# Second MLP's weight words through ScalarE's leaky step, and a shorter reach for the written-out order

## The chip, the cores and the metric

The kernel runs on one core of one Trainium2 chip. The metric is the time of the whole program on the device, in microseconds (us), from the first instruction to the last write. Five engines work beside each other, each through its own queue in order: PE (TensorE, with its weight loads shown as PEld), DVE (VectorE), ACT (ScalarE), POOL (GpSimd) and SP (SyncE, which issues nearly all DMAs here).

## What is computed

Causal attention with a decay bias (4 batches, 8 heads, 576 positions, 64 per head), then two MLPs over its 2304 tokens, each 512 wide with 2048 in the middle. The first has a softplus in the middle, the second a quotient of two polynomials.

```python
x = attention(q, k, v, s)                    # 2304 x 512, fp32
h = x @ moe_w_in;  g = softplus(h);  x = g @ moe_w_out
h = x @ moe2_w_in
P = a0 + a1*h + a2*h*h + a3*h*h*h
Q = 1 + |b0|*|h| + |b1|*h*h
out = (P / (Q + 1e-6)) @ moe2_w_out
```

The four weight matrices come as 64-bit floats, so the kernel reads pairs of 32-bit words and builds fp32 values from them on the chip. All matrix products are made in three passes of a shorter format: a value is split into a high part (a rounded copy) and a low part (the value less its high part), and high by high, high by low and low by high are summed in PSUM.

## The kernel before

**Stages.** From 0 to about 200 us attention for the first tokens and the building of the first MLP's weights share the engines. Then the first MLP runs (token tiles T1 of 256 and 448 columns, 16 units of 128 middle rows each) with the rest of attention woven in, to about 625 us. The second MLP follows: its first tile (384 tokens) plainly, three tiles of 512 with a scheme that saves one product in eight, and the last tile (TAIL, 384 tokens) plainly again, from about 962 us to the end.

**A unit** of an MLP is `stage_a` (12 matmuls, x by the in-weights, L1095 to L1097), `stage1` to `stage3` (the function on ACT, DVE and POOL, ending with the high part `gh` on ACT and the low part `gl` on POOL, both seen as L1391 and L1393) and `stage_b` (the out-weights into `acc`, L1131 to L1133 in the first MLP, L1138 to L1140 in the second). In the first MLP L1197 is the DVE step that frees the PSUM bank of `h` in the tiles meant here; in the second it is L1209.

**Building weights.** `load_w` fetches 128 x 512 pairs of words. `conv_t(m, ff, half)` turns them into fp32 in a tile `tc` (three buffers), m is 0 for the first MLP's weights and 1 for the second's. `conv_hl` then takes the high part on ACT (L921) and the low part on POOL (L922). There are 32 such conversions for each MLP. Those of the second MLP are issued by `conv2_a` and `conv2_b` during units 65 to 96, which is the last two tiles of the first MLP and the start of the second; for each pair of converted in-weights `sum_make` (L986 to L989, four DVE steps) and `sum_split` (L997 on ACT, L998 on POOL) make and store sums that the saving scheme needs. Twelve of the 32 (the in-weights' half of units 0 to 11) go into buffers of the tag W, which the first MLP's last tile frees unit by unit.

For m = 0 the conversion is a DVE shift of the low word (L910), one ACT step (Prelu, which scales by one factor above zero and by another below, L911) on the high word in place, and one DVE step that shifts and joins (L912). For m = 1 it is a scaling on POOL in place (L914) and three DVE steps (L915, L916, L917). For either, the first step on the loaded words waits for the load.

**Order.** The program is traced in a hand-made sequence with priorities. Before the framework schedules it, a planner in the kernel (`Step`, `Planner`, `plan`) lays all instructions out over the engines with its own table of durations, six rounds by turns of start and due times, takes the round that ends soonest, and ties each engine's instructions into that order. `plan` leaves out of the ties every instruction whose planned start is at or after `UNTIL`, on the planner's own clock, which the trace doesn't show. With 2000.0 nothing is left out. What is left out keeps its data waits and its priority, and the framework places it.

Of the kernel before, what the change touches and what calls it, by code (L numbers as in the profile page):

```python
# [11 lines left out]
AF = mybir.ActivationFunctionType  # L12
ALU = mybir.AluOpType
# [52 lines left out]
SHARED = {("two", "wide"): 0.7, ("two", "thin"): 0.25, ("one", "wide"): 0.7, ("one", "thin"): 0.3,  # L66
          ("wide", "two"): 0.2, ("wide", "one"): 0.05, ("thin", "two"): 0.6, ("thin", "one"): 0.3}
HOLD, ROUNDS = 0.0, 6
UNTIL = 2000.0
DMA_RATE, DMA_LATENCY, LANES = 320e3, 1.9, 8  # L70


# [252 lines left out]
def plan(instructions, tied, until):  # L325
    p = Planner(instructions, tied)
    rank = [s.i.bass_priority for s in p.steps]
    best = None
    for _ in range(ROUNDS):
        total = p.forward(rank)  # L330
        if best is None or total < best[0]:
            best = total, p.lines, p.start
        rank = p.latest()
    _, lines, start = best
    return [[p.steps[k].i for k in line if start[k] < until] for line in lines.values()]
# [3 lines left out]
def moe_chain_kernel(ctx, tc, qk0, v0, qk, vv, s0, s, w1, w2, ab, out):  # L339
    nc = tc.nc  # L340
# [558 lines left out]
    def conv(m, ff, half, hi, lo):  # L899
        conv_hl(conv_t(m, ff, half), hi, lo)  # L900

    def conv_t(m, ff, half):
        r = raw64.pop((m, ff, half))
        lw = r[:, :, 0]
        hf = r.bitcast(F32)[:, :, 1]
        hw = r[:, :, 1]
        t = sb.tile([128, 512], F32, tag="tc", bufs=3, name="tc")
        ti = t.bitcast(I32)
        if m == 0:
            nc.vector.tensor_scalar(ti, lw, 29, None, op0=ALU.logical_shift_right)  # L910
            nc.scalar.activation(hf, hf, AF.Prelu, scale=2.0 ** -112, alpha=-(2.0 ** 32))  # L911
            nc.vector.scalar_tensor_tensor(ti, hw, 3, ti, op0=ALU.logical_shift_left, op1=ALU.bitwise_or)  # L912
        else:
            nc.gpsimd.tensor_scalar(hf, hf, 2.0 ** -112, 1.0, op0=ALU.mult, op1=ALU.mult)  # L914
            nc.vector.tensor_scalar(ti, hw, 3, None, op0=ALU.logical_shift_left)  # L915
            nc.vector.scalar_tensor_tensor(ti, hw, -2147483648, ti, op0=ALU.bitwise_and, op1=ALU.bitwise_or)  # L916
            nc.vector.scalar_tensor_tensor(ti, lw, 29, ti, op0=ALU.logical_shift_right, op1=ALU.bitwise_or)  # L917
        return t

    def conv_hl(t, hi, lo):  # L920
# [27 lines left out]
    def conv2_a(ff, half):  # L948
        t = conv_t(1, ff, half)
        c2_open.append((conv2_hl, (ff, half, t)))  # L950
        if half == 0:
            q, p = ff // 4, ff // 2 % 2
            pairs.setdefault((q, p), []).append(t)
            if ff % 2:
                pairs[q, p].append(sb.tile([128, 512], F32, tag="tc", bufs=3, name="tc"))
                c2_open.append((sum_make, (q, p)))
                c2_next.extend((sum_split, (q, p, n)) for n in range(2))
# [659 lines left out]

    for line in plan(nc.cur_bb.bb.instructions, tied, UNTIL):
        for prev, i in zip(line, line[1:]):
# [59 lines left out]
```

## Time and profile before

| | us |
|---|---|
| three runs | 1047.83, 1048.87, 1049.39 (median 1048.87) |
| the profiled execution, its own time | 1048.41 |
| its span in the trace | 1046.6 |
| PE busy in the span | 1005.5 |
| DVE busy | 846.5 |
| ACT busy | 785.6 |
| POOL busy | 506.7 |

The profiled execution lies 0.46 us below the median of the three, and its time is 1.8 us longer than its span. Busy times are those of the engine itself; waiting isn't in them. PE's busy time counts a matmul as busy also while it runs at the lower of its two clock levels, which the granted clock shows (1.00 is full speed, 0.50 the lower level).

### The profile page before, as it was taken

The numbers are of one execution on the slowest core, as the hardware profiler recorded it, in microseconds if no ns is written. First come the engines' busy times: TensorE is split into PE (matmuls) and PEld (weight loads), VectorE is DVE, ScalarE is ACT, GpSimd is POOL, SyncE is SP. The second block draws the span as 40 slices with busy tenths as digits, with TensorE's granted clock in tenths as the row PEclk, the third lists the DMA queues.
The fourth block names the chain that finished last, engine by engine and source line by source line (L and its number), as shares of the span: only waits on it lengthen the run. The fifth ranks groups of instructions, "written<-read, shape, count | busy, mean of one in ns | idle before, by whom it ended". The sixth has DMA issues, their size and how long they took to land. (4 is left out here: it accounts for less than half of the span.)

```text
span 1046.6 us, 18293 instructions
## 1 busy us (share of the span) xinstructions
PE 1005.5 (96%) x5924; PEld 902.2 (86%) x5924; DVE 846.5 (81%) x1815; ACT 785.6 (75%) x1620; POOL 506.7 (48%) x496
## 2 busy tenths in 40 slices
PE   6999999999999999999999978899999999999997
PEld 5889999989998888889999968688888898899895
DVE  5788987888987888886667899898889878878866
ACT  5998888887987777766566555778778888788765
POOL 2757654311211122234437876676567457455542
PEclk9999999999999999999999999999999999999999
DMA  8868565665555644337689987967645655654300
GB/s 242 299 237 274 180 223 178 201 196 153 169 179 153 203 138 152 97 136 235 215 261 332 330 276 255 357 215 271 195 162 186 215 181 175 201 175 147 121 1 31
DMA packets 103503, 207.93 MB, mean 199 GB/s; under 512 B 11632, under 2 KB 28848, under 8 KB 103408
## 3 DMA queue, kind: packets, MB, share of 16 engines
q1 hardware_dynamic: 100864, 202.60, 58.6%
q10 hardware_dynamic: 2544, 4.16, 1.6%
q8 instruction: 47, 0.77, 0.3%
q14 instruction: 48, 0.39, 0.1%
HBM read 163.25 MB, written 39.39 MB: 194 GB/s over the span
## 5 line engine op out<-in xcount | busy, mean ns | idle before, releaser
L616 POOL TENSOR_SCALAR PA<-PA,stat 128x384 f32<-128x384 f32 (+3 forms) x112 | 73.1, 659 | 164.0 <-DVE stat L615 64.8
L1095 PE MATMUL h<-xs,w1h 128*128 128x448 f32 (+1 forms) x360 | 123.1, 343 | 3.8 <-DVE e L1197 3.7
L1096 PE MATMUL h<-xs,w1h 128*128 128x448 f32 (+1 forms) x360 | 122.7, 341 | 0.0
L1097 PE MATMUL h<-xs,w1l 128*128 128x448 f32 (+1 forms) x360 | 122.3, 340 | 0.0
L1132 PE MATMUL acc<-gl,w1h 128*128 128x448 f32 (+1 forms) x352 | 119.1, 340 | 1.2 <-POOL gl L1393 1.2
L1133 PE MATMUL acc<-gh,w1l 128*128 128x448 f32 (+1 forms) x352 | 118.8, 340 | 0.1
L1131 PE MATMUL acc<-gh,w1h 128*128 128x448 f32 (+1 forms) x352 | 118.9, 341 | 0.0
L1260 POOL TENSOR_TENSOR gl<-PA,gh 128x512 fp32r<-128x512 f32 x48 | 63.7, 1328 | 70.1 <-issue 57.3
L613 ACT ACTIVATE PA<-PA,stat 128x384 f32<-128x384 f32 (+3 forms) x112 | 64.0, 572 | 16.2 <-DVE stat L596 14.1
L1095 PEld LDWEIGHTS h<-xs,w1h 128*128 128x128 f32 x360 | 67.9, 189 | 9.0 <-DVE e L1197 5.7
L1096 PEld LDWEIGHTS h<-xs,w1h 128*128 128x128 f32 x360 | 67.8, 188 | 3.7 <-DVE xs L1060 0.4
L1097 PEld LDWEIGHTS h<-xs,w1l 128*128 128x128 f32 x360 | 67.8, 189 | 3.2
L1132 PEld LDWEIGHTS acc<-gl,w1h 128*128 128x128 f32 x352 | 66.4, 189 | 4.6 <-POOL gl L1393 1.4
L1133 PEld LDWEIGHTS acc<-gh,w1l 128*128 128x128 f32 x352 | 66.2, 189 | 3.4 <-POOL w1l L922 0.3
L1131 PEld LDWEIGHTS acc<-gh,w1h 128*128 128x128 f32 x352 | 66.3, 189 | 3.1 <-ACT gh L1391 0.2
L1193 ACT ACTIVATE e<-h 128x448 f32<-128x448 f32 (+1 forms) x90 | 43.4, 482 | 32.2 <-PE h L1097 29.2
L1393 POOL TENSOR_TENSOR gl<-e,gh 128x256 fp32r<-128x256 f32 (+1 forms) x48 | 47.6, 992 | 29.9 <-ACT gh L1391 24.7
L1276 PE MATMUL acc<-w2b,gl 128*128 128x512 f32 x144 | 55.5, 397 | 2.0 <-POOL gl L1260 2.0
L1274 PE MATMUL acc<-w2b,gh 128*128 128x512 f32 x144 | 56.8, 394 | 0.0
L1275 PE MATMUL acc<-w2b,gh 128*128 128x512 f32 x144 | 56.7, 394 | 0.0
L596 DVE CUSTOM_DVE_ANT_0 PA<-at,mask 128x384 f32<-128x384 f32 (+3 forms) x100 | 50.4, 518 | 5.9 <-PE at L624 3.9
L623 PE MATMUL at<-ht 128*128 128x512 f32 (+3 forms) x156 | 53.5, 348 | 1.1 <-DVE stat L604 0.8
(362 smaller groups left out, 3325.8 us busy)
## 6 DMA issues: line engine op xcount, KB each, us to landing
wa<-wa_d SPq DMA_DIRECT2D x100, 512.0 KB
w1l<-l_d SPq DMA_DIRECT2D x138, 256.0 KB
raw<-in_w_dram SPq DMA_DIRECT2D x48, 512.0 KB
raw<-in_qk_dram SPq DMA_DIRECT2D x24, 384.0 KB
l_d<-w1l SPq DMA_DIRECT2D x32, 256.0 KB
raw64x<-in_w_dram SPq DMA_DIRECT2D x16, 512.0 KB
wa_d<-pt SPq DMA_DIRECT2D x16, 512.0 KB
wa_d<-w2a SPq DMA_DIRECT2D x24, 256.0 KB
```

Of the source, the lines that this page charges most:

```text
L613: nc.scalar.activation(pt[:, 0:n], pt[:, 0:n], AF.Exp, bias=mn, scale=-1.0, accum_out=stat[:, i, 1:2])
L616: nc.gpsimd.tensor_scalar(pt[:, 0:n], pt[:, 0:n], stat[:, i, 2:3], 1.0, op0=ALU.mult, op1=ALU.mult)
L1095: nc.tensor.matmul(h, wh[:, cs], xh, start=(k == 0), stop=False)
L1096: nc.tensor.matmul(h, wh[:, cs], xl, start=False, stop=False)
L1097: nc.tensor.matmul(h, wl[:, cs], xh, start=False, stop=(k == KD - 1))
L1131: nc.tensor.matmul(o, wh[:, cs], gh, start=first and not both, stop=False)
L1132: nc.tensor.matmul(o, wh[:, cs], gl, start=False, stop=False)
L1133: nc.tensor.matmul(o, wl[:, cs], gh, start=False, stop=last and (not both or m % 2 == 1))
L1260: nc.gpsimd.tensor_tensor(gl, bl.g, f(gh), op=ALU.subtract)
L1274: nc.tensor.matmul(acc[m], gh[:, cs], wh, start=first, stop=False)
L1275: nc.tensor.matmul(acc[m], gh[:, cs], wl, start=False, stop=False)
L1276: nc.tensor.matmul(acc[m], gl[:, cs], wh, start=False, stop=last)
```

## The change

`conv_t` loses its second branch: the weights of both MLPs are now converted as the first MLP's were. For each of the 32 conversions of the second MLP one POOL step and three DVE steps go, and two DVE steps and one ACT step come. `UNTIL` becomes 936.0, so that instructions which the planner starts at 936 us of its clock or later (nearly all of the last tile) are no longer tied in its order. The planner runs again over the changed list of instructions, so the order of the rest may change as well.

```diff
-UNTIL = 2000.0
+UNTIL = 936.0
...
-        if m == 0:
-            nc.vector.tensor_scalar(ti, lw, 29, None, op0=ALU.logical_shift_right)
-            nc.scalar.activation(hf, hf, AF.Prelu, scale=2.0 ** -112, alpha=-(2.0 ** 32))
-            nc.vector.scalar_tensor_tensor(ti, hw, 3, ti, op0=ALU.logical_shift_left, op1=ALU.bitwise_or)
-        else:
-            nc.gpsimd.tensor_scalar(hf, hf, 2.0 ** -112, 1.0, op0=ALU.mult, op1=ALU.mult)
-            nc.vector.tensor_scalar(ti, hw, 3, None, op0=ALU.logical_shift_left)
-            nc.vector.scalar_tensor_tensor(ti, hw, -2147483648, ti, op0=ALU.bitwise_and, op1=ALU.bitwise_or)
-            nc.vector.scalar_tensor_tensor(ti, lw, 29, ti, op0=ALU.logical_shift_right, op1=ALU.bitwise_or)
+        nc.vector.tensor_scalar(ti, lw, 29, None, op0=ALU.logical_shift_right)
+        nc.scalar.activation(hf, hf, AF.Prelu, scale=2.0 ** -112, alpha=-(2.0 ** 32))
+        nc.vector.scalar_tensor_tensor(ti, hw, 3, ti, op0=ALU.logical_shift_left, op1=ALU.bitwise_or)
         return t
```

## Rows read from the trace of the kernel before

**Rows 1.** The page's first part: busy us, share of the span, instructions.

```profile
PE 1005.5 (96%) x5924; PEld 902.2 (86%) x5924; DVE 846.5 (81%) x1815; ACT 785.6 (75%) x1620; POOL 506.7 (48%) x496
```

**Rows 2.** Busy us by stretch: length, PE, PEld, DVE, ACT, POOL, granted clock, DMA.

```profile
590.00:660.00 70.00, 59.95 (x288) 53.24 (x287) 65.54 (x79) 38.44 (x74) 50.00 (x41) 0.98 0.81 274
660.00:720.00 60.00, 56.27 (x290) 47.47 (x289) 52.57 (x75) 46.88 (x90) 43.53 (x35) 1.00 0.75 266
0.00:200.00 200.00, 183.52 (x1309) 170.40 (x1310) 162.68 (x494) 162.50 (x406) 113.75 (x138) 1.00 0.70 227
200.00:560.00 360.00, 359.39 (x2043) 324.20 (x2042) 282.16 (x768) 266.53 (x581) 97.68 (x125) 1.00 0.58 183
...
963.00:1032.00 69.00, 69.00 (x345) 61.90 (x343) 54.45 (x82) 49.90 (x96) 34.88 (x32) 1.00 0.15 49
```

**Rows 3.** PE's waits, 560 to 660: for whom, us, times, longest.

```profile
PE h L1095 <- DVE e L1197: 5.3, 4, 3.1
PE h L1095 <- DVE PA L1209: 2.7, 3, 1.7
PE acc L1138 <- ACT gh L1391: 1.9, 1, 1.9
```

**Rows 4.** PE's longest gap of these (timeline), and two stretches after it.

```profile
621.91 0.45 PE L1095 MATMUL h<-yt,w2a 128*128 128x384 f32 x1 [3.09 <-DVE e L1197]
...
622.00:624.00 2.00, 2.00 (x8) 1.90 (x9) 2.00 (x2) 1.94 (x5) 1.86 (x3) 0.68 1.01 376
624.00:626.00 2.00, 2.00 (x8) 1.87 (x7) 2.00 (x4) 1.05 (x2) 2.00 (x3) 0.50 0.95 337
```

**Rows 5.** DVE's groups by line, 590 to 660: count, busy us, mean ns.

```profile
L916 DVE SCALAR_TENSOR_TENSOR tc<-raw,tc 128x512 int32<-128x512 int32 x5 | 6.3, 1255 | 0.1
L917 DVE SCALAR_TENSOR_TENSOR tc<-raw64x,tc 128x512 int32<-128x512 int32 x5 | 5.4, 1080 | 0.1
L915 DVE TENSOR_SCALAR tc<-raw64x 128x512 int32<-128x512 int32 x5 | 5.1, 1021 | 0.0
...
L916 DVE SCALAR_TENSOR_TENSOR tc<-raw64x,tc 128x512 int32<-128x512 int32 x5 | 4.4, 885 | 0.1
...
L917 DVE SCALAR_TENSOR_TENSOR tc<-raw,tc 128x512 int32<-128x512 int32 x5 | 3.7, 741 | 0.1
...
L915 DVE TENSOR_SCALAR tc<-raw 128x512 int32<-128x512 int32 x5 | 3.6, 723 | 0.7 <-POOL raw L914 0.7
```

**Rows 6.** Single lines: groups 0 to 200, then whole span as min/median/max ns.

```profile
L912 DVE SCALAR_TENSOR_TENSOR tc<-raw,tc 128x512 int32<-128x512 int32 x32 | 27.5, 860 | 2.0 <-ACT raw L911 1.8
L910 DVE TENSOR_SCALAR tc<-raw 128x512 int32<-128x512 int32 x32 | 20.8, 656 | 2.8 <-POOL w1l L922 2.1 <-DMA raw<-in_w_dram 0.6
...
L911 ACT ACTIVATE raw<-raw x32: 646/667/694, 20.9 to 190.7; 128x512 f32<-128x512 f32 x32
...
L916 DVE SCALAR_TENSOR_TENSOR tc<-raw,tc x16: 674/833/1776, 410.8 to 641.1; 128x512 int32<-128x512 int32 x16
```

**Rows 7.** POOL: L914 by stretch (us, count), and its waits 390 to 660.

```profile
590.00:660.00 70.00, 6.64 (x8) 0.98 0.81 274
...
POOL raw L914 <- DMA raw<-in_w_dram: 20.3, 7, 8.2
POOL raw64x L914 <- DMA raw64x<-in_w_dram: 7.9, 6, 2.3
```

**Rows 8.** The end: PE's waits from 1000, then PE's and ACT's timeline.

```profile
PE acc L1138 <- ACT gh L1391: 2.4, 3, 1.0
PE acc L1140 <- POOL gl L1393: 0.8, 2, 0.4
...
1029.84 0.34 PE L1097 MATMUL at<-xl,wa 128*128 128x384 f32 x1
...
1030.22 0.71 ACT L1205 ACTIVATE tmp<-e,prm 128x384 f32<-128x384 f32 x1
1032.48 0.52 ACT L1391 ACTIVATE gh<-PA 128x384 fp32r<-128x384 f32 x1 [1.54 <-DVE PA L1222]
...
1033.97 0.47 ACT L1204 ACTIVATE e<-at 128x384 f32<-128x384 f32 x1
```

## Prediction, written before the changed kernel was run

> **What bounds the kernel now.** I read the busy times of the whole span first, then the same by stretch, then PE's waits in the stretches where PE is not full, then the engine that it waits for there. PE is busy 96% of the span, DVE 81%, ACT 75%, POOL 48% [rows 1], so the program as a whole is PE's, and a change that takes no matmul away can give back only PE's idle time and its time at the lower clock. By stretch [rows 2] PE is full from 200 to 560 (359.39 of 360 us) and from 963 to 1032 (69.00 of 69). It is idle at the start (16.5 us of the first 200), from 590 to 660 (70 less 59.95, 10.05 us), from 660 to 720 (3.73 us) and at the very end. In 590 to 660 another engine is the full one: DVE is busy 65.54 of 70 us, while ACT has 31.6 us free and POOL 20. PE's waits there name DVE: 5.3 us for L1197 and 2.7 us for L1209, the DVE steps that free the PSUM bank of h, and 1.9 us for a gh that itself stands behind DVE's L1222 [rows 3]. That makes 9.9 of the 10.05 us. After the longest gap, 3.09 us, the granted clock falls: 0.68 in the next 2 us and 0.50 in the 2 us after them [rows 4], which is the lower level of 1.2 GHz in place of 2.4. Together (2 x 0.32 + 2 x 0.50) this is 1.64 us of lost work beside the idle time. So what DVE's lateness costs from 590 to 660 is about 11.7 us, and this is the stretch in which ten of the 32 conversions run.
>
> **The conversion, DVE's part.** In this stretch ten conversions cost DVE 6.3 + 5.4 + 5.1 + 4.4 + 3.7 + 3.6 = 28.5 us [rows 5], 2.85 us each. The new form is in the trace already, for the first MLP: L912 27.5 and L910 20.8 us over 32 [rows 6], 48.3 / 32 = 1.51 us each, in a stretch in which POOL is busy 57% [rows 2]. In 590 to 660 POOL is busy 71%, and 62% once its 6.64 us for L914 are gone [rows 7], so 1.51 us fits. The upper bound of the relief is then 10 x (2.85 - 1.51) = 13.4 us. The lower bound is one undisturbed two-input step for each conversion, 0.674 us, the least of L916 [rows 6]: 6.7 us. Between them lies how much of DVE's lengthening (L916 takes 0.674 us at the least and 1.776 at the most for one shape) goes away with L914. I take a relief of 10 us, nearer to the first MLP's rows since they are the same two instructions beside the same POOL work.
>
> The Trainium skill (SBUF — State Buffer, section Who interferes with whom) says that DVE steps with two SBUF inputs and GpSimd steps lock each other out for a whole instruction. The lengths of L916 agree. By this rule L914's 6.64 us come off DVE's waiting at the most; with the 6.7 us of the removed step that would be 13.3 us, an estimate that meets the upper bound above.
>
> **What of that reaches PE.** DVE with 55 us of work in 70 would no longer be full, and PE's work there takes 59.95 us, some 58.3 at full clock. Not all idle goes: the steps still come in bursts (the four steps of the sums beside two conversions, then L1197), and the banks of h give PE little slack. I take 70% of the 10.05 us, 7.0 us. The lower clock came behind the longest gap; if that gap shrinks as the others do, most of the 1.64 us comes back, and I take 1.5. What comes late next is DVE still, at a lower load, then POOL's low parts and sums (43 us in 70). From 660 to 720 no conversion is left, but a smaller backlog enters it; of its 3.73 us I take none, and 1 us as a bound.
>
> **ACT's part.** 32 Prelu steps of 0.667 us [rows 6], 21.3 us. L911 varies from 646 to 694 ns although it stands between the attention's and the softplus' functions, so no table is switched for it. Ten fall into 590 to 660, 6.7 us against 31.6 us free; the others fall into a stretch where ACT is busy 266.53 of 360 us [rows 2]. I cost them at nothing as work: ACT's free time hides them, and if that cover were gone each 0.667 us would stand before an Abs, Exp or Ln of a unit. What they can cost is a wait. The first step on a loaded word pair waits for the load: POOL waited 20.3 us in 7 times and 7.9 us in 6 for it, once 8.2 us [rows 7]. This wait now stands in ACT's queue (and DVE's, whose first step reads the same load), with gh and the function steps of the first MLP behind it, for which PE waits. Bounds: 0 (the planner puts the step where the load has landed) and 8.2 us (the longest wait passed on whole). PE is full where these loads are made and units lie three deep between `stage_a` and `stage_b`, so a wait of a microsecond or two is covered; I take 1 us.
>
> The Trainium skill (ScalarE: Activation LUTs, rules for kernel authors) says to do relu and multiplications on VectorE and not on ScalarE. The rows show next to no difference for one step of this size: 0.667 us for L911, 0.656 us in the mean for the one-input L910 on DVE beside POOL's work [rows 6]. By the rule the scaling would go to DVE, ten such steps in the stretch where DVE is full; the relief would shrink by 6.6 us, and at 70% of it the time would be 1041 + 4.6 = 1045.6 us.
>
> **POOL's part.** 32 steps leave POOL. POOL is not full anywhere PE waits, so by itself this is worth nothing; its effect on DVE is counted above. One POOL wait moves: its low parts no longer queue behind L914.
>
> **The last tile.** From 963 to 1032 PE is full in the planner's order. Then it waits 2.4 us for gh and 0.8 us for gl [rows 8], 3.2 us. One cause is visible: the last unit's matmuls are issued by 1029.84 + 0.34, ACT ends its queue's work at about 1030.9, then waits for the gh of an earlier unit until 1032.48, and takes the last unit's Abs (L1204) only at 1033.97. Another order could take that Abs some 3 us earlier. So the bound on the good side is 3.2 us, and on the bad side there is none in the trace, since every instruction of it was tied; I bound it by letting each of the 16 units wait as the first late one does at the end (1.0 us, the longest for gh, and 0.4 for gl, half of the two waits): 16 x 1.4 = 22 us. DVE (54.45 of 69), ACT (49.90) and POOL (34.88) have time there, so any order that keeps three units in flight leaves PE full, and I take 0.
>
> **Sum.** Against the profiled execution: 1048.41 - 7.0 - 1.5 + 1.0 + 0 = 1040.9 us. The median lies 0.46 us above this execution: 1041.4, and I say 1041.
>
> **Rivals.** (a) The relief is there but little of it reaches PE: low parts, the sums on POOL, or the buffers of the tag W (freed unit by unit by the first MLP's last tile) hold the conversions, and PE's waits keep their size under other names. For it: POOL waits for ACT there as ACT does for DVE, a chain in which one link is shortened. Against it: 9.9 of 10.05 us of PE's waits name DVE directly or one step away. It would give a third of the 8.5 us: 1048.9 - 2.8 = 1046. (b) Nothing to measure: the planner lays the whole program out anew from a changed list, and what is gained from 590 to 660 is lost in the first 200 us, which hold 16.5 us of idle time in an order that would change, or in the last tile: 1047 to 1051. (c) Slower, by the last tile: the framework places a unit's `stage_b` on PE before its gl is there, and the next `stage_a` stands behind it in PE's queue. Its place is 963 to 1043, its price up to 1.4 us a unit, and from 8.5 / 1.4 = 6 late units on it eats the gain; with all 16 late the time is 1041 + 22 = 1063. Against it: DVE, ACT and POOL have a fifth to a half of their time free there. (d) Slower, by ACT's queue: three or more Prelu steps wait for loads as long as POOL's 8.2 us once did, with PE's gh behind them. Beyond a cover of some 5 us each (a guess: PE lost 0.61 us in all from 200 to 560 although POOL had that wait there) this is 3 x 3.2 = 10 us: 1051. (e) More than forecast: all 11.7 us, 1 us from 660 to 720 and 3.2 at the end: 1033. (f) That the change doesn't do what it says, with the leaky step slower than its rows or the planner keeping POOL's order, I leave out: the same function on the same shape runs 32 times in this trace.
>
> **How the numbers follow.** A measurement of this kernel can tell about 0.2%, 2.1 us, so "same" is 1046.8 to 1051.0. Chances: the forecast (1036 to 1044.5) 0.50; (a) 0.12; (b) 0.17; (c) 0.13; (d) 0.05; (e) 0.03. Faster is 0.50 + 0.12 + 0.03 = 0.65, same 0.17, slower 0.18. The range from 1034 to 1051 takes in the forecast, (a), (b) and the bounds of the relief, and leaves out (c), (d) beyond its start and the far end of (e), together about 0.2.
>
> **What would show it.** Right: from 590 to 660 DVE's busy time falls by about 10 us, the conversion's DVE lines cost about 1.5 us per conversion, PE's waits for L1197 and L1209 fall below 3 us together, and the clock stays at 1.00. ACT's L911 then counts 64, POOL's L914 none. Wrong in the relief: DVE stays above 63 of 70 us. Wrong in its reach: DVE has time and PE still waits there, for POOL or ACT. Wrong in ACT: long waits of L911 for loads with PE's waits for gh near them. Wrong in the last tile: PE gaps between 963 and 1032, or more than 3.2 us behind.

## The result, and the profile after

The changed kernel takes 1036.74 us (median of four, 1035.87 to 1037.39) against 1049.01 for the kernel before in the same comparison: a ratio of 0.9884, 95% interval 0.9867 to 0.9902, or 12.3 us less. The forecast was 1041 and its range 1034 to 1051. The profiled execution took 1037.39 us and its span is 1035.6.

PE's matmuls are the same 5924 in both. The conversion's lines L910 to L912 are L909 to L911 in the changed kernel, and all line numbers behind `conv_t` are six lower. The page's first part, busy us, share of the span and instructions, of the changed kernel:

```profile
PE 1002.6 (97%) x5924; PEld 902.5 (87%) x5924; DVE 814.8 (79%) x1783; ACT 803.7 (78%) x1652; POOL 477.5 (46%) x464
```

Beside [rows 1] DVE lost 32 instructions and 31.7 us, ACT gained 32 and 18.1 us, POOL lost 32 and 29.2 us. By stretch, in the columns of [rows 2]:

```profile
0.00:200.00 200.00, 183.82 (x1309) 170.20 (x1309) 161.46 (x494) 162.38 (x406) 113.62 (x138) 1.00 0.69 227
200.00:560.00 360.00, 359.43 (x2046) 324.88 (x2045) 271.69 (x753) 277.12 (x602) 80.62 (x105) 1.00 0.59 183
...
590.00:660.00 70.00, 65.19 (x320) 58.97 (x318) 58.22 (x76) 50.34 (x96) 50.17 (x38) 0.98 0.90 308
660.00:720.00 60.00, 56.84 (x308) 48.50 (x306) 53.46 (x74) 46.99 (x89) 41.43 (x34) 1.00 0.80 278
```

The first 560 us are as they were. In 590 to 660 DVE fell from 65.54 to 58.22 us, ACT took 11.9 us more and PE's idle time halved, from 10.05 to 4.81 us. PE's waits from 560 to 660, against 9.9 us in [rows 3]:

```profile
PE h L1089 <- DVE PA L1203: 2.2, 1, 2.2
PE h L1089 <- DVE e L1191: 1.8, 2, 1.4
PE at L1089 <- DVE PA L1203: 0.8, 1, 0.8
```

Since the work moves in time, stretches of equal times don't hold equal work. A better measure is the start of PE's k-th matmul in either trace, k counted in order of start (from 0; counting from 1 moves a number by some 0.2 us). In us, worked out from the traces:

```
k           1200   2400   3450   3900   4800   5400   end of span
before     184.0  384.2  580.3  686.6  840.4  938.0  1046.6
after      184.8  384.5  579.9  678.2  831.2  928.7  1035.6
lead        -0.8   -0.3    0.4    8.4    9.2    9.3    11.0
```

Nearly all of it comes in three parts: 8.0 us between the 3450th and the 3900th matmul (580 to 687 us before the change), where the conversions lie, 0.8 us in the 150 us behind that, and 1.7 us in the last tile, between its first matmul and the end. The 450 matmuls of the first part have the same shapes in both kernels. While they run, PE's idle time falls from 11.6 to 5.2 us and DVE's busy time from 94.1 to 80.9 us.

### The profile page after: what moved, and what is told of

Same layout as the page of the kernel before. It is cut to its first block, busy times and chain, and to the rows that moved or that the text cites. A ratio compares the mean times of both kernels' runs of the same rounds, so it can differ in the third digit from the quotient of the medians.

```text
span 1035.6 us, 18274 instructions
## 1 busy us (share of the span) xinstructions
PE 1002.6 (97%) x5924; PEld 902.5 (87%) x5924; DVE 814.8 (79%) x1783; ACT 803.7 (78%) x1652; POOL 477.5 (46%) x464
## 4 chain that ended last, share of the span: by engine, by line
PE 62%; DVE 15%; ACT 9%; issue 5%; POOL 4%; DMA 4%; SPq 0%; DVEq 0%; POOLq 0%; ACTq 0%
PE at L764 5%; PE h L1089 5%; PE h L1090 5%; PE h L1091 5%; PE acc L1127 4%; PE acc L1125 4%; PE acc L1126 4%; PE at L1330 4%; PE h L1330 3%; PE acc L1270 3%; PE at L623 2%; PE acc L1269 2%; PE acc L1268 2%; PE at L624 2%; DVE tc L911 2%
```

## Experiments

**The two parts apart.** First the shorter reach alone, then the leaky conversion alone.

```diff
-UNTIL = 2000.0
+UNTIL = 936.0
```

> The shorter reach of the written-out order alone (UNTIL 936), the second MLP's conversion as before. Theory: the two parts of the change add up. By PE's matmul starts compared rank by rank, the changed kernel was 9.3 us ahead of the kernel before when the last tile began and 11.06 us at the last matmul, so the last tile's order is worth 1.7 us: 1049.0 - 1.7 = 1047.3, with nothing changed before about 960 us and PE's gaps behind 1029 us cut from 3.2 us to 0.4, against one new gap near 979. Rival: the last tile's gain comes from what the changed conversion leaves behind (another arrival of the loads and sums), then this run is level with the kernel before, 1049 +- 0.5, and keeps the 3.2 us.

Measured: 1049.1 us beside 1048.98, ratio 1.0001 (0.9992 to 1.001). The gain of 1.7 us did not come, so the theory failed; the time is the rival's, but not for the rival's reason, since the end's wait did go. The trace says why; PE's waits from 970 to 1000 in this kernel, and then those from 1000 to its end:

```profile
PE acc L1138 <- ACT yb L1279: 1.8, 1, 1.8
PE acc L1138 <- DVE yb L1280: 0.3, 1, 0.3
...
PE acc L1138 <- ACT gh L1391: 0.4, 1, 0.4
```

The end's 3.2 us of [rows 8] fell to 0.4 as expected, but the free order opened a new gap of 2.1 us at the handover: PE waits there for the copies of the previous tile's results, which the planner's order had earlier. From the last tile's first matmul to the end of the last matmul the trace gives 79.5 us against 80.5 before, and the times can't tell 1 us from nothing.

The other half is the kernel after with `UNTIL = 2000.0`.

> The leaky conversion alone, all instructions tied in the planner's order as before (UNTIL 2000). Theory that the parts add up: 9.3 us of the gain, 1049.0 - 9.3 = 1039.7, the last tile with some 3.2 us of gaps at its end as in the kernel before. Rival that they need each other: 1037 or 1043 and more.

Measured: 1039.29 us, ratio 0.9908 (0.9895 to 0.9922), 9.7 us less, as expected. PE's waits from 940 to the end are the kernel before's to the tenth:

```profile
PE acc L1132 <- ACT gh L1385: 2.4, 3, 1.0
PE acc L1134 <- POOL gl L1387: 0.8, 2, 0.4
```

By the times the conversion is worth 9.7 us, and the shorter reach 2.55 us behind it but nothing without it. By the traces of the last tile the shorter reach is worth 2.1 us behind the conversion (80.9 to 78.8 us) and 1.0 us without it. The handover's gap, 1.4 us in the changed kernel and 2.1 us in the shorter reach alone, makes 0.7 us of this difference, and the rest lies within the spread of the runs.

**Which part of the conversion.** Two kernels change one thing each, both with `UNTIL = 2000.0`. In the first the scaling goes from POOL to ACT and DVE keeps three steps:

```diff
-            nc.gpsimd.tensor_scalar(hf, hf, 2.0 ** -112, 1.0, op0=ALU.mult, op1=ALU.mult)
+            nc.scalar.activation(hf, hf, AF.Prelu, scale=2.0 ** -112, alpha=1.0)
             nc.vector.tensor_scalar(ti, hw, 3, None, op0=ALU.logical_shift_left)
             nc.vector.scalar_tensor_tensor(ti, hw, -2147483648, ti, op0=ALU.bitwise_and, op1=ALU.bitwise_or)
             nc.vector.scalar_tensor_tensor(ti, lw, 29, ti, op0=ALU.logical_shift_right, op1=ALU.bitwise_or)
```

> Only the engine of the scaling is changed: the second MLP's high words are scaled on ACT (Prelu with a slope of 1 on both sides, the same instruction in cost) and no longer on POOL; DVE keeps its three steps. UNTIL 2000. Theory that the step taken off DVE carries the gain: here DVE gets only what POOL's 6.64 us between 590 and 660 had lengthened, at most 6.6 us, likely a third: 1049 - 2 to 3 = 1046.5. Rival that POOL's steps, by lengthening DVE's, were the cost: most of the 9.3 us, 1041 to 1043.

In the second POOL keeps the scaling and DVE makes two steps; this kernel leaves out the weights' sign, so its time serves for comparison only:

```diff
         nc.vector.tensor_scalar(ti, lw, 29, None, op0=ALU.logical_shift_right)
-        nc.scalar.activation(hf, hf, AF.Prelu, scale=2.0 ** -112, alpha=-(2.0 ** 32))
+        if m == 0:
+            nc.scalar.activation(hf, hf, AF.Prelu, scale=2.0 ** -112, alpha=-(2.0 ** 32))
+        else:
+            nc.gpsimd.tensor_scalar(hf, hf, 2.0 ** -112, 1.0, op0=ALU.mult, op1=ALU.mult)
         nc.vector.scalar_tensor_tensor(ti, hw, 3, ti, op0=ALU.logical_shift_left, op1=ALU.bitwise_or)
```

> Only DVE's third step is taken away: the scaling of the second MLP's high words stays on POOL, and DVE makes the two steps of the new form. The weights lose their sign with that, which is the part of the computation left out. UNTIL 2000. Theory that the step taken off DVE carries the gain: two thirds or more of the 9.3 us, 1049 - 6.5 = 1042.5. Rival that POOL's steps were the cost: a third, 1046.

Measured: 1046.37 us with the scaling on ACT (ratio 0.9981, 0.9972 to 0.999) and 1044.21 us with two steps (0.9956, 0.9943 to 0.997): 2.6 and 4.8 us less, 9.7 with both. By the times the step taken off DVE is the larger part, but it is half of the gain and not two thirds, and the two together give 2.3 us more than their sum. From 590 to 660, first the scaling on ACT, then the two steps (columns as in [rows 2]):

```profile
590.00:660.00 70.00, 63.07 (x298) 57.26 (x297) 60.97 (x79) 45.24 (x86) 45.55 (x34) 0.93 0.87 283
```

```profile
590.00:660.00 70.00, 63.19 (x306) 56.67 (x304) 59.66 (x75) 42.44 (x81) 52.32 (x44) 0.98 0.92 305
```

Either takes DVE down from 65.54, by 4.6 and by 5.9 us, and PE's idle time from 10.05 to 6.93 and 6.81. The same over equal work, the 450 matmuls from the 3450th to the 3900th, worked out from the traces in us ("lost to the clock" is the length times the clock share that was not granted):

```
                             before   scaling on ACT   two steps   changed
length                        106.3        104.6         101.4       98.3
PE idle                        11.6          8.8           7.6        5.2
lost to the clock               1.7          5.1           1.7        1.7
DVE busy                       94.1         91.0          85.9       80.9
ten conversions, DVE steps     28.5         31.2          19.7       20.7
one DVE step of the sums       1.02         0.79          0.92       0.79
```

Two things follow. With the scaling on ACT, PE lost 3.4 us more to the lower clock than in the other kernels. Without that the two halves would be level here, and 3.4 us is more than the 2.3 us that the sum falls short by; so which half is larger isn't shown. Each kernel also has an order of its own, and the next experiment shows that orders alone differ by more than 2.3 us. And taking L914 away didn't make the conversion's own steps cheaper: the ten cost DVE 31.2 us in place of 28.5. It was the steps of the sums that got shorter.

**What an order is worth.** The planner makes a new order for every list of instructions. These two kernels change no instruction of the kernel before, only one number of the planner's table:

```diff
-        return self.after[k] + LATENCY.get((a, b), 0.04)
+        return self.after[k] + LATENCY.get((a, b), 0.05)
```

> The kernel before with one number of the planner's table changed (the latency between engines 0.05 in place of 0.04 us on its clock), so that the whole order is made anew by a slightly different reckoning and no instruction changes. It measures what a new order by itself does. Theory that the gain came from work taken off DVE: this stays within 2 us of the kernel before, 1047 to 1051. Rival that orders differ by luck as much as the change moved: 3 us or more to either side.

Measured: 1053.63 us, ratio 1.004 (1.0028 to 1.0052), 4.9 us more. The rival holds: orders differ by half of what the change moved. But the place is another one. In 0 to 200 PE is busy 179.99 us, 3.5 less than in [rows 2], from 200 to 560 another 3.7 less, and in 590 to 660 it is no worse:

```profile
0.00:200.00 200.00, 179.99 (x1283) 166.82 (x1284) 157.52 (x483) 159.57 (x399) 113.96 (x136) 1.00 0.68 220
...
590.00:660.00 70.00, 61.29 (x297) 55.11 (x296) 64.67 (x78) 39.51 (x75) 55.52 (x44) 0.98 0.81 272
```

A single comparison could then have been luck, so the conversion was tried in other orders too: 0.05 and 0.03 for both forms of it, `UNTIL = 2000.0` throughout.

> The leaky conversion, UNTIL 2000, with the planner's latency at 0.05: the partner of the kernel before with 0.05, which took 1053.6. That one lost its 4.9 us before 500 us, where no conversion of the second MLP matters yet. Theory that the conversion gains by work taken off DVE between 580 and 690, whatever the order: about 9.7 us less than its partner, 1044, with PE's lead over its partner made between these two times. Rival that the gain lay in the one order that the planner found for it: less than half of that, 1049 or more.

> The kernel before with the planner's latency at 0.03, a third order of the same instructions. With 1049.0 (0.04) and 1053.6 (0.05) it shows the spread of orders. Theory: a spread of 3 to 5 us, from the first 500 us above all; 1046 to 1054. Rival that the order of 0.04 was picked and is the best by far: 1053 or more.

> The leaky conversion with 0.03, the partner of the run before this. Theory: 6 to 12 us less than its partner. Rival (luck of one order): less than 4 us less, or more.

Measured, with the time from the 3300th to the 3900th matmul of each trace beside it:

```
planner's latency     0.04      0.05      0.03
three DVE steps    1048.98   1053.63   1055.55 us    136.8   135.1   137.9 us
leaky conversion   1039.29   1041.41   1046.75 us    128.2   125.8   128.5 us
difference             9.7      12.2       8.8         8.6     9.3     9.4
```

Two of these expectations missed. The kernel before with 0.03 makes the spread of its three orders 6.6 us, wider than the theory's 3 to 5, and the rival's number came (1053 or more): in either form the order of 0.04 is the fastest of the three. And of the 12.2 us with 0.05, more than the 9.7 expected, 9.3 lie in the stretch. With 0.03 the pair differs as expected.

With the old conversion three orders spread over 6.6 us and with the new one over 7.5 us, and yet the pairs differ by 8.8 to 12.2 us, and in the stretch of the conversions by 8.6 to 9.4. So in all three orders the conversion gains about 9 us there. What differs between orders lies elsewhere: with the old form in the first 200 us above all, where both new orders keep PE busy only 180 of them; with the new form and 0.03 mostly behind the conversions, where it falls 6 us further behind the order of 0.04.

**The scaling on DVE.** The rule that the prediction cited, multiplications on VectorE, here with DVE's three steps kept:

```diff
-            nc.gpsimd.tensor_scalar(hf, hf, 2.0 ** -112, 1.0, op0=ALU.mult, op1=ALU.mult)
+            nc.vector.tensor_scalar(hf, hf, 2.0 ** -112, 1.0, op0=ALU.mult, op1=ALU.mult)
```

> The scaling of the second MLP's high words on DVE (one more one-input step for each conversion, four in all) in place of POOL, UNTIL 2000: what a rule that keeps multiplications on VectorE would do with the scaling. Theory that DVE is the bound from 590 to 660: the step adds 4 to 6.6 us of DVE work there, of which about 70% reaches PE, less what leaving POOL gave (2.6 us with the scaling on ACT): 1049.0 + 1 to 2 = 1050.5. Rival that lock-outs by POOL weigh more than DVE's own steps: 1046 to 1047, as with the scaling on ACT.

Measured: 1050.53 us, ratio 1.0016 (1.0005 to 1.0026), 1.8 us more: the time that was expected. DVE, from 560 to 590 and from 590 to 660 (65.54 us before), then the scaling's own durations in ns (least, median, most):

```profile
560.00:590.00 30.00, 30.00 (x147) 27.59 (x148) 28.04 (x36) 20.13 (x38) 22.45 (x16) 1.00 0.99 348
590.00:660.00 70.00, 61.36 (x297) 54.85 (x296) 66.56 (x87) 38.98 (x75) 45.10 (x34) 0.98 0.85 288
```

```profile
L914 DVE TENSOR_SCALAR raw<-raw x16: 409/424/1508, 408.6 to 630.0; 128x512 f32<-128x512 f32 x16
L914 DVE TENSOR_SCALAR raw64x<-raw64x x16: 412/426/844, 453.6 to 644.7; 128x512 f32<-128x512 f32 x16
```

The place is not the one expected. From the 3450th to the 3900th matmul DVE is busy 97.7 us against 94.1 before, and yet PE takes 104.7 us for them against 106.3. What this kernel loses it loses in front of them (3.4 us between the 2400th and the 3450th matmul) and behind them (1.1 us). So DVE's busy time alone doesn't set PE's waits. It must matter which of DVE's steps come late, but no run here separates that.

With the same three steps kept, the scaling on ACT gives 1046.4 and on DVE 1050.5. The step itself is shorter on DVE, 0.42 us in the median and 0.53 in the mean against 0.667 on ACT [rows 6]. That is the direction of the rule of the Trainium skill (ScalarE: Activation LUTs, rules for kernel authors), but the kernel is no faster by it. The difference of 4 us is below the spread of orders, so it isn't shown either that ACT is the better place.

**The last tile.** Two kernels look at it. One is the changed kernel with `UNTIL = 955.0`; the other keeps 936 and frees ACT's queue alone:

```diff
-    return [[p.steps[k].i for k in line if start[k] < until] for line in lines.values()]
+    return [[p.steps[k].i for k in line if p.steps[k].engine != "Activation" or start[k] < until] for line in lines.values()]
```

> The changed kernel with UNTIL 955 in place of 936. Its last tile has two gaps on PE: 1.36 us at 970, where PE waits for DVE's copy of the previous tile's results (L1274) that the planner's order had earlier, and 0.40 us at the end, where the planner's order has 3.2 us. With 955 the handover from the tile before stays tied and only the second half of the last tile is free. Theory that these are two separate places: no gap at the handover, 0.4 at the end, 1036.7 - 1.4 = 1035.4. Rival that the end's order pays only because of what the free handover leaves: the end's gaps come back to 2 to 3 us, 1037 to 1039.

> The leaky conversion, with UNTIL 936 for ACT's queue alone; PE, DVE, POOL and SP stay tied to the end. Theory that the end's 3.2 us come from ACT taking the last unit's first step (Abs, L1198) behind an earlier unit's gh: the framework takes that Abs first, the end's gaps shrink to 1 us or less and the time is that of the changed kernel or a little under, 1035.5 to 1037. Rival that the tied order of PE and DVE carries the end: 3 us of gaps stay and the time is that of the conversion alone, 1039.3.

Measured: 1034.5 us with 955 (ratio 0.9855, 0.984 to 0.9869) and 1036.12 us with ACT alone free (0.9869, 0.9855 to 0.9884). Both go as the theories said, the first 0.9 us lower. PE's waits from 940 to the end, in this order: the changed kernel, 955, ACT alone free.

```profile
PE acc L1132 <- DVE yb L1274: 1.4, 1, 1.4
PE acc L1132 <- ACT gh L1385: 0.4, 1, 0.4
```

```profile
PE acc L1132 <- ACT gh L1385: 0.4, 1, 0.4
```

```profile
PE acc L1133 <- ACT gh L1386: 0.5, 1, 0.5
PE acc L1133 <- ACT yb L1274: 0.3, 1, 0.3
```

The end's 3.2 us go when ACT's order alone is freed, so it was ACT's order. The handover's 1.4 us is a price of freeing too early; at 955 it isn't paid. That kernel is the fastest measured here, 2.2 us below the changed one.

**A further relief of DVE.** The same kernel with two copies of the first MLP's last results on ACT:

```diff
+            elif (ph, T) == (0, 5):
+                nc.scalar.activation(yb[:, 1], i, AF.Copy)
             else:
                 nc.vector.tensor_copy(yb[:, 1], i)
```

> The changed kernel with UNTIL 955 (1034.5 us) and the two copies of the first MLP's last results that DVE makes (0.61 us each, near 645 us) moved to ACT, which has 20 of 70 us free there. Theory that DVE is still what PE waits for there (2.2 us for L1203 behind the gap at 645): 1.2 us less DVE work, 0.5 to 1 us gained, 1033.5 to 1034. Rival that the two copies also hold PSUM banks and are later in ACT's queue, or that the new order hides the effect: 1034.5 to 1036.

Measured: 1036.03 us (1033.34 to 1036.44), ratio 0.9875 (0.9857 to 0.9894), against 0.9855 (0.984 to 0.9869) without it. No gain: the theory failed, and the time is the rival's upper end. DVE did fall in its profiled execution, from 58.00 to 56.58 us, and PE's busy time rose from 64.55 to 65.66 of 70:

```profile
590.00:660.00 70.00, 65.66 (x326) 58.94 (x326) 56.58 (x77) 51.74 (x100) 48.40 (x38) 1.00 0.90 310
```

That execution was also the fastest of its four, the others 2.5 to 3.1 us longer, so the trace doesn't show what the others lost. This stays open.

## Why the prediction was right, and where its terms were off

**What bounds the kernel** was read rightly: from 590 to 660 PE waits for DVE. All that the conversion gave came there or just behind, and in three orders it came to nearly the same amount. One row was read too closely: the gh of 1.9 us stood behind ACT's L1204, which had waited 2.08 us for DVE's L1221, and not behind L1222. It is DVE in either case.

Most of the signs that were named for being right did not come in full. ACT's leaky step counts 64 and POOL's L914 none, as said. But DVE's busy time from 590 to 660 fell by 7.3 us and not by 10, a conversion costs 2.06 us of DVE and not 1.5, PE's waits there are 4.8 us and not under 3, and the clock fell once. The range held although several terms were off.

**The relief of DVE** was put at 10 us for ten conversions, between 6.7 and 13.4. Measured, the ten conversions in the changed kernel's 580 to 650 cost (DVE's groups by line, columns as in [rows 5])

```profile
L911 DVE SCALAR_TENSOR_TENSOR tc<-raw64x,tc 128x512 int32<-128x512 int32 x5 | 6.9, 1381 | 0.2
L909 DVE TENSOR_SCALAR tc<-raw64x 128x512 int32<-128x512 int32 x5 | 6.0, 1204 | 5.9 <-POOL pt L992 5.8
L911 DVE SCALAR_TENSOR_TENSOR tc<-raw,tc 128x512 int32<-128x512 int32 x5 | 5.6, 1128 | 1.0 <-ACT raw L910 0.9
...
L909 DVE TENSOR_SCALAR tc<-raw 128x512 int32<-128x512 int32 x5 | 2.1, 418 | 0.0
```

together 20.6 us, 2.06 us each and not 1.51, so on the conversions the relief was 28.5 - 20.6 = 7.9 us. This part was too large because it took the mean of the first MLP's rows. The five conversions of `raw` do cost 1.5 us each; the five of `raw64x` cost 2.6. DVE's timeline shows a pair, then POOL's what ran beside it:

```profile
595.18 0.42 DVE L909 TENSOR_SCALAR tc<-raw 128x512 int32<-128x512 int32 x1
595.70 0.69 DVE L911 SCALAR_TENSOR_TENSOR tc<-raw,tc 128x512 int32<-128x512 int32 x1
...
600.19 1.51 DVE L909 TENSOR_SCALAR tc<-raw64x 128x512 int32<-128x512 int32 x1 [3.26 <-POOL pt L992]
...
602.15 1.25 DVE L911 SCALAR_TENSOR_TENSOR tc<-raw64x,tc 128x512 int32<-128x512 int32 x1
```

```profile
598.87 2.54 POOL L992 TENSOR_TENSOR pt<-tc,pt 128x512 fp32r<-128x512 f32 x2
601.38 1.47 POOL L916 TENSOR_TENSOR w2a<-tc,w2a 128x512 fp32r<-128x512 f32 x1
```

Of the 20 steps each one that took 1.2 us or more overlaps a POOL step, and those with nothing on POOL beside them took 0.42 to 0.43 us (L909) or 0.68 to 0.69 (L911). So the lengths go with what POOL does beside each step; the share of the stretch in which POOL is busy, by which the prediction chose its rows, didn't tell them.

On the other side the prediction left out the sums. Their DVE steps, which the edit doesn't touch, fell from 1.02 to 0.79 us each. Over the 450 matmuls DVE's busy time fell by 13.2 us in all, some 3 us of it three steps of the sums that moved out of the stretch.

The estimate of 13.3 us from the Trainium skill (SBUF — State Buffer, section Who interferes with whom) meets that total, but not for its reason. The lengths agree with it in kind: L911, with two inputs in SBUF, took 0.69 us with POOL idle and 1.25 beside POOL's steps. But with L914 gone and nothing else (the scaling on ACT) the ten conversions cost no less, 31.2 us, and DVE's busy time on the same matmuls fell by 3.1 us, where 6.64 was the most that L914 could give.

**What reaches PE** was put at 70% of the idle time, 7.0 us. Over the 450 matmuls PE's idle time fell by 6.4 us, and PE got through them 8.0 us sooner; the other 1.6 us lie in PE's busy time, some of it because there are fewer gaps: behind the gap at 645.83 the second matmul starts 0.28 us after the first, where matmuls of this shape in an unbroken row start 0.17 us apart. Of the 13.2 us that DVE lost, a share of about 0.6 came through. In the other two orders it was 9.1 us of 15.8 and 9.1 of 17.9. So the share was about right. That the product came near is luck in part, since the relief it rests on was put together from other steps. Another 0.8 us came behind the stretch, where the prediction took none and 1 us as a bound.

**The clock** was to give back 1.5 us. In the changed kernel's profiled execution it gave nothing: a gap of 2.23 us is left, and behind it the clock falls as in [rows 4]. PE's timeline, then two stretches (columns as in [rows 2]):

```profile
645.83 0.44 PE L1089 MATMUL h<-yt,w2a 128*128 128x384 f32 x1 [2.23 <-DVE PA L1203]
```

```profile
646.00:648.00 2.00, 2.00 (x8) 2.00 (x9) 1.90 (x5) 1.02 (x2) 0.00 (x0) 0.58 1.00 241
648.00:650.00 2.00, 2.00 (x8) 1.61 (x7) 1.93 (x3) 2.00 (x5) 1.73 (x2) 0.57 1.08 391
```

That is 2 x 0.42 + 2 x 0.43 = 1.7 us of lost work, as before. The term was not wrong in kind. In the other profiled executions with the full new conversion the clock is 0.98 from 590 to 660 in two (the conversion alone, and with ACT alone free) and 1.00 in four (0.05, 0.03, `UNTIL = 955.0`, and the same with the copies on ACT). In none of the seven of the other kernels is it above 0.98 there. The stretch in the orders of 0.05 and 0.03:

```profile
590.00:660.00 70.00, 66.20 (x331) 59.84 (x330) 57.25 (x76) 50.06 (x96) 49.90 (x39) 1.00 0.93 319
590.00:660.00 70.00, 65.15 (x322) 58.06 (x321) 57.82 (x75) 47.48 (x91) 47.24 (x37) 1.00 0.90 299
```

**ACT's wait for loads** was put at 1 us and cost nothing. The leaky steps of both MLPs in the changed kernel, then the only wait for a load that ACT had before them:

```profile
L910 ACT ACTIVATE raw<-raw x48: 653/667/706, 20.7 to 633.7; 128x512 f32<-128x512 f32 x48
L910 ACT ACTIVATE raw64x<-raw64x x16: 647/664/676, 454.3 to 638.6; 128x512 f32<-128x512 f32 x16
...
  DMA raw<-in_w_dram: 0.7, 1
```

The steps last what [rows 6] said, and that one wait lies at 167.7 us, in the first MLP's weights; the second MLP's 32 steps waited for no load. So rival (d) fell. Why POOL waited 28.2 us for loads [rows 7] and ACT not at all isn't shown; in another order it did (3.8 us in 7 times, with the scaling on ACT and three steps on DVE). The price that came in its place wasn't named: from 390 to 660 DVE waited for ACT's step 8 times, 6.3 us, against 1.3 us in 2 for POOL's L914. Only 0.9 us of that lies in the stretch of 580 to 650 where DVE is short of time.

**The last tile** was put at 0, with 3.2 us as the bound on the good side. By the trace it gave 1.7 us in the changed kernel, by the medians 2.55 beside the conversion alone. The sign of this part had been left open; the mechanism that the rows showed was the right one. ACT's and PE's timeline in the changed kernel:

```profile
1023.24 0.49 ACT L1198 ACTIVATE e<-at 128x384 f32<-128x384 f32 x1 [0.38 <-PE at L1091]
```

```profile
1022.87 0.34 PE L1091 MATMUL at<-xl,wa 128*128 128x384 f32 x1
```

The last unit's Abs starts 0.03 us after its last matmul, against 3.8 us in [rows 8]. What was missed is the handover, a gap between 963 and 1032 us, which the prediction had named as a sign of being wrong: rival (c) looked for lost time in every unit of the tile, and it came once, before the tile's results could begin to gather, since the copies of the tile before were free to move as well.

**Rival (b)**, the new order, was priced at a loss in the first 200 us; here these changed by 0.3 us of PE's busy time. That was luck as far as the runs show: four more orders moved the whole kernel by 2 to 7.5 us, all to the slower side. The sum had no term for it, and the range's width covered it only because it reached to the rivals.

Taken together, between the two profiled executions 11.0 us were gained against a sum of 7.5. The stretch of the conversions gave 8.0 against 8.5 (idle time and clock). Three terms make the difference: the last tile, put at 0, gave 1.7; ACT's wait, put at a cost of 1, cost nothing; and the time behind the stretch, put at 0, gave 0.8. Another 0.4 us came before the 3450th matmul. The median came out 4.3 us below the forecast: 3.5 us from these terms, and 0.7 because the changed kernel's profiled execution is 0.65 us slower than its median.

## What to carry to other kernels

Where one engine is nearly full and names most of the bound engine's waits, a part of what is taken off it comes through (here a share of 0.5 to 0.6), and its busy time alone doesn't tell which part. Compare the same work before and after, not the same times, and count all steps of the relieved engine: here steps that the edit doesn't touch got shorter too. What a step costs depends on what runs beside it, so a mean from another stretch can mislead. Where instructions are reordered with every edit, measure what an order is worth (here up to 7.5 us) before a gain of that size is put down to the edit, and repeat the pair in other orders. When a hand-made order is loosened, look at both ends of the loosened part: here one end won 2.8 us and the other lost 1.4 to 2.1.

## What the runs showed of the hardware that was not expected

A gap of PE of the same length, at the same place, was followed by the lower clock in one execution and not in another. In the changed kernel 2.23 us without a matmul were followed by 0.58 and 0.57 (above). The conversion alone and the kernel with ACT alone free had the same gap, 2.19 and 2.21 us, and the lower clock behind it (0.57 from 645 to 649 in both). In the kernel with 955, whose order differs from the changed kernel's only in the last tile, PE's timeline and the next stretches are

```profile
644.63 0.44 PE L1089 MATMUL h<-yt,w2a 128*128 128x384 f32 x1 [2.21 <-DVE PA L1203]
```

```profile
645.00:647.00 2.00, 1.65 (x10) 1.32 (x8) 1.90 (x5) 1.21 (x3) 0.00 (x0) 1.00 0.97 280
647.00:649.00 2.00, 1.55 (x7) 1.31 (x8) 1.93 (x3) 2.00 (x5) 1.94 (x2) 1.00 1.09 388
```

and the clock stays at 1.00. What decides between them no run here shows. It makes 1.7 us, but it doesn't explain by itself how the runs of one kernel spread: of the changed kernel's four, the one with a mean granted clock of 1.000 took 1036.39 us and one with 0.999 took 1035.87, and of the conversion's alone the one with 1.000 is the slowest (1039.72).
